# Smaller GpSimd pieces, half-tile turns of x and a fourth result buffer in a fused two-attention kernel

## The chip, the cores and the metric

The kernel runs on one core of one Trainium2 chip. A core has TensorE (PE in the profile), VectorE (DVE), ScalarE (ACT), GpSimd (POOL) and SyncE (SP), which here issues all DMAs. The metric is the device time of one execution in microseconds. The kernel before took 917.41 us, the median of three runs (917.04 to 918.87).

## The reference, cut to what matters

One input x (2048 rows of 512, bfloat16) goes through two attentions of 32 heads with 16 columns each, and a gate mixes them:

```
g = sigmoid((x * gate_w).sum(-1))
a = softmax(q k^T / 4) v @ wo            # full attention, weights A
b = softmax over 8 keys at distance 0, 2, .. 14, then @ wo    # local, weights B
out = g * a + (1 - g) * b
```

Both q, k and v come from x @ wqkv, with weights of their own. Part a needs 32 x 2048 x 2048 exponentials; part b only 32 x 2048 x 8.

## The kernel before, in words

**Loading and turning x.** x comes in four tiles of 512 rows (`load_x`), A's weights after the first tile. TensorE turns each x tile (`tr`, 16 transposes of 128 x 128, eight in each half of the columns) into PSUM, and two copies bring it to SBUF as `xTs[0]` and `xTs[1]` (`ev`: the first half on ScalarE, the second on VectorE). The PSUM tile `pxt` of an x tile takes 4 KB of a partition, in place `rA` for the even tiles and `rB` for the odd.

**PSUM.** Its eight banks are named: `rA` (three banks) and `rB` (two), the two score rings; `acc` (one), the running result of part a; and two `misc` banks, which every other product passes through.

**Part a.** The work is cut in 32 periods: a block of 512 queries (`c_`) and a group of four heads (`i`). A period has 64 units (16 key blocks of 128 times four heads), each a score tile of 128 keys x 512 queries. Three to five units of a period (`n_dve`) get their exponential on VectorE, the rest on ScalarE, in sets of three and two units by turns: `qk` writes the scores of a set into ring `rA` or `rB`, `ex` takes the exponential of the whole set into a `pT` buffer, and `pv` multiplies it with V and adds to `acc`, for two sets at a time (`pairs`). `pT` has three buffers a ring (`p_bufs`). K of a group is projected by `k_proj` and its row maxima taken (`km`) and joined (`selk`); q of a period by `q_proj`; V by `v_proj`. For group 0 ScalarE copies K (`kc`), otherwise VectorE. At a period's end VectorE transposes `acc` (`po1`), divides by the row sums and transposes back.

**VectorE's exponential.** `d_group` takes units one or two together. For each, `chain_of` has a score matmul into `misc` (`dq`) and four VectorE steps, `p1` to `p4`: `p1` writes `dt` (two buffers), `p2` reads `dt` twice (misc<-dt in the profile), `p3` and `p4` follow, and `p4` writes a `pd` tile of two units (four buffers), which is freed when its `pv` has read it.

**Part b.** For each of 16 blocks of 128 rows, `b_tile` projects q, k, v, writes k and v to DRAM and reads eight shifted copies of each back (`ksh`, `vsh`). GpSimd then multiplies and adds in a buffer `prod`: `logits_half` twice, then softmax on VectorE and ScalarE, then `av_half` twice. Its pieces are at most `HB` = 512 columns. The blocks are due 46.7 us apart (`b_space`), beginning at 32 us (`b_start`).

**The order.** Every step is an `op` with an engine, an estimated length, a due time, the steps that it depends on and the buffers that it takes and uses (`tok`). `list_schedule` plays these out once, when the program is built, and gives each engine a fixed order; PSUM banks and buffers go by that plan. An engine runs its order strictly in sequence, so a step that is held holds those behind it. The planner also puts filler matmuls of zeros (`zero`, the rows acc<-ones_t,z) where TensorE would be idle for long in its plan (`COVER`, `SPAN`). `rel` is a time in the plan before which a step does not start.

**The end.** The two results are projected with wo, mixed and written out in tiles of 128 rows; the last four wait for the last period.

All instructions but TensorE's carry one line, 280 (the helper that chains an engine's order); matmuls have 289, the turns of x 480. So the readings go by tile names.

Of the kernel before, what the change touches and what calls it, by code (L numbers as in the profile page):

```python
# [9 lines left out]
ALU = mybir.AluOpType  # L10
# [8 lines left out]
    set_sizes=(3, 2),  # L19
    n_dve=(3,) * 2 + (4,) * 14 + (5,) * 16,  # L20
    dve_tiles=2,
    p_bufs=3,
    pairs=True,
    cover=0.68,
    force=1.0,
    d_slack=2.0,
    d_lead=4.0,
    d_early=5.0,
    pd_bufs=4,
    q_bufs=3,  # L30
    shift=6.0,
    hold=0.3,
# [19 lines left out]
QW = 512  # L52
# [168 lines left out]
def kernel(  # L221
# [46 lines left out]
    def chain(bi):  # L268
        return chain_on("pe", bi)
# [199 lines left out]
    o_xt = []  # L469
    for sc in range(NC):  # L470
        st = {}
        tk = tok("rA" if sc % 2 == 0 else "rB", 1)

        def tr(half, sc=sc, st=st):
            def s():
                if half == 0:
                    st["p"] = ps.tile([128, DC, QW], BF16, tag=("rA" if sc % 2 == 0 else "rB"), bufs=1, name="pxt")
                for c in range(2 * half, 2 * half + 2):
                    for tt in range(TPC):
                        chain(nc.tensor.transpose(out=st["p"][:, c, tt * 128:(tt + 1) * 128],  # L480
                                                  in_=xld[sc][:, tt, c * 128:(c + 1) * 128], identity=ident[:]))
            return s

        def ev(half, sc=sc, st=st):
            def s():
                dst = xTs[half][:, :, sc * QW:(sc + 1) * QW]
                src = st["p"][:, 2 * half:2 * half + 2, :]
                if half == 0:
                    A.copy(out=dst, in_=src)
                else:  # L490
                    V.tensor_copy(out=dst, in_=src)
            return s
        t1 = op("pe", 0.6, tr(0), -5.0 + sc, deps=[o_x[sc], o_id], alloc=[tk], use=[xtok[sc]])
        t2 = op("pe", 0.6, tr(1), -4.9 + sc, deps=[t1], use=[tk, xtok[sc]])
        o_xt.append([op("act", 1.0, ev(0), -5.0 + sc, deps=[t1], use=[tk]),
                     op("dve", 0.68, ev(1), -4.9 + sc, deps=[t2], use=[tk])])
    all_xt = [o for os_ in o_xt for o in os_]


# [14 lines left out]
    def k_proj(i, sc, tag, dl, rel=0.0):  # L514
        st = {}
        tk = tok(tag, 2 if tag == "misc" else 1)

        def part(c0, c1):
            def s():
                if c0 == 0:  # L520
                    st["pk"] = misc_ps([128, QW], tag=tag)
                for c in range(c0, c1):
                    mm_heads(st["pk"], c, 1, i, xTs[c // 2][:, c % 2, sc * QW:(sc + 1) * QW], c == 0, c == DC - 1)
            return s

        def kc():
            if i == 0:
                A.activation(out=kt_all[:, i, sc * QW:(sc + 1) * QW], in_=st["pk"][:], func=ACT.Identity, scale=rowc[:, 0:1],
                             bias=rowc[:, 1:2])
                return  # L530
            V.tensor_scalar(out=kt_all[:, i, sc * QW:(sc + 1) * QW], in0=st["pk"][:], scalar1=rowc[:, 0:1],
                            scalar2=rowc[:, 1:2], op0=ALU.mult, op1=ALU.add)

        def km():
            V.tensor_reduce(out=kmax_all[:, i, sc:sc + 1], in_=st["pk"][:], axis=AX.X, op=ALU.max,
                            apply_absolute_value=True)
        b = steps(part, tk, dl - 2.6, [o_two[1, min(i, 1)], o_init_d] + o_xt[sc], rel=rel, name=f"kp{i}.{sc}")[-1]
        if i == 0:
            o_kc0.append(op("act", 0.65, kc, dl, deps=[b, o_init_d], use=[tk]))
            return op("dve", 0.70, km, dl, deps=[b], use=[tk])  # L540
        c = op("dve", 0.81, kc, dl - 0.8, deps=[b], use=[tk])
        return op("dve", 0.70, km, dl, deps=[b, c], use=[tk])

    def selk(i, dl):
        def s():
            V.tensor_reduce(out=kmax[:, i:i + 1], in_=kmax_all[:, i, :], axis=AX.X, op=ALU.max)
            V.scalar_tensor_tensor(out=rowq[:, i:i + 1], in0=kmax[:, i:i + 1], scalar=rowc[:, 2:3], in1=rowc[:, 0:1],
                                   op0=ALU.mult, op1=ALU.add)
        o_selk[i] = op("dve", 0.40, s, dl, deps=o_kc[i])

    for i in range(NG):
# [35 lines left out]
            for t in range(tb, tb + TB):  # L587
                o_v[(h, t)] = c

    v_proj(0, 4, 0, 8, "acc", T0 + 2.0, rel=T0 - 2.0)  # L590
    v_proj(0, 4, 8, 8, "misc", T0 + 3.0, rel=T0 - 2.0)
    for h0, h1, pn in ((4, 8, 2), (8, 16, 4), (16, 24, 8), (24, 32, 12)):
        TB = 512 // ((h1 - h0) * DH)
        for tb in range(0, NT, TB):
# [35 lines left out]
        c = op("dve", 0.70, mg, dl - 0.8, deps=[b], use=[tk])  # L630
        o_q[pi] = op("dve", 0.80, ev, dl, deps=[c, o_selk[i]], use=[tk, tq])

    q_proj(0, "misc", 2.9)
    for pi in range(1, NP):
        q_proj(pi, "misc", S0[pi] - 8.0 - shift(pi), rel=S0[pi - 1] - 1.0 - shift(pi))

# [46 lines left out]
    o_kvd, o_obt = [], []  # L683
    obt_tiles, obt_tok = {}, {}
    WH = W // 2
    HB = D

    def b_tile(t):
        st = {}
# [101 lines left out]
        def av_half(hf):  # L791
# [23 lines left out]
                    if hf:  # L815
                        G.tensor_tensor(out=st["obb"][:, cs], in0=ob[:, cs], in1=prod[:, 0, cs], op=ALU.add)
            return s
        l0 = op("pool", 11.9, logits_half(0), tb + 8, deps=[lk, qa], alloc=[tlg], use=[tks, tqb], name=f"lg{t}")
        l1 = op("pool", 11.9, logits_half(1), tb + 18, deps=[l0], use=[tks, tqb, tlg])
        a = op("dve", 1.3, sm_pre, tb + 19, deps=[l1], use=[tlg])  # L820
        a = op("act", 0.45, sm_exp, tb + 18, deps=[a], use=[tlg])
        a = op("dve", 2.28, sm_post, tb + 21, deps=[a, o_g], use=[tlg])
        a0 = op("pool", 10.2, av_half(0), tb + 40, deps=[a, lv], alloc=[tob], use=[tlg, tvs])
        a1 = op("pool", 11.8, av_half(1), tb + 48, deps=[a0], alloc=[tbb], use=[tlg, tvs, tob])
        tk = tok("misc", 2)
        if cb not in obt_tok:
            obt_tok[cb] = tok("obt", 2)
# [115 lines left out]
    def d_group(pi, gr, lo, hi):  # L943
        c_, i = periods[pi]
        n = len(gr)
        st = {}
        tp = tok("pd", cfg["pd_bufs"])

        def chain_of(q_, t, j, dl):
            tx, td = tok("misc", 2), tok("dt", 2)  # L950

            def dq():
                st["x"] = ps.tile([128, QW], FP32, tag=f"misc{bank[0]}", bufs=1, name="misc")
                mm(st["x"][:], kt_all[32 * j:32 * j + 32, i, t * 128:(t + 1) * 128], qt_tiles[pi][32 * j:32 * j + 32, :],
                   True, True, tile_position=(32 * j, 0))

            def p1():
                st["dt"] = work.tile([128, QW], FP32, name="dt", tag="dt", bufs=2)
                V.tensor_scalar(out=st["dt"][:], in0=st["x"][:], scalar1=float(DH) ** -0.5 * BITS / LN2,
                                scalar2=127.0 * BITS, op0=ALU.mult, op1=ALU.add)  # L960
                st["fr"] = st["dt"][:].bitcast(U16).rearrange("p (n two) -> p n two", two=2)[:, :, 0]

            def p2():
                V.scalar_tensor_tensor(out=st["x"][:], in0=st["fr"], scalar=EXP_A, in1=st["fr"],
                                       op0=ALU.subtract, op1=ALU.mult)

            def p3():
                V.scalar_tensor_tensor(out=st["x"][:], in0=st["fr"], scalar=EXP_R, in1=st["x"][:],
                                       op0=ALU.add, op1=ALU.mult)

            def p4():
                if q_ == 0:
                    st["pd"] = work.tile([128, 2, QW], BF16, name="pd", tag="pd", bufs=cfg["pd_bufs"])
                V.scalar_tensor_tensor(out=st["pd"][:, q_, :].bitcast(U16), in0=st["x"][:], scalar=EXP_C,
                                       in1=st["dt"][:], op0=ALU.mult, op1=ALU.add)
            a = op("pe", 0.20, dq, dl - 3.6, rows=True, deps=[o_q[pi], o_kc[i][t // TPC] if i else o_kc0[t // TPC]],
                   after=[d_last[0]], alloc=[tx], use=[q_tok[pi]], rel=lo, lat=0.47, name=f"dq{pi}")
            a = op("dve", 0.70, p1, dl - 2.3, deps=[a], alloc=[td], use=[tx])
            a = op("dve", lambda t_: 1.0 if in_b(t_) else 0.72, p2, dl - 1.4, deps=[a], use=[td, tx])
            a = op("dve", 0.70, p3, dl - 0.7, deps=[a], use=[td, tx])  # L980
            d_last[0] = op("dve", 0.70, p4, dl, deps=[a], alloc=[tp] if q_ == 0 else [],
                           use=[td, tx] + ([tp] if q_ else []), slack=cfg["d_slack"])

        def pv():
            for q_, (t, j) in enumerate(gr):
                pv_mm(pi, t, j, st["pd"][:, q_, :], vp_all[:, t])
        for q_, (t, j) in enumerate(gr):
            chain_of(q_, t, j, hi - 1.0 - 3.5 * (n - 1 - q_))
        a = d_last[0]
        o_pv[pi].append(op("pe", 0.23, pv, max(hi, S0[pi] + 5.0), deps=[a, o_t0[pi]] + [o_v[(4 * i + j, t)] for t, j in gr],  # L990
                           use=[tp, acc_tok[pi]], name=f"dpv{pi}",
                           sums=[((pi, j_), sum(1 for x in gr if x[1] == j_), NT) for j_ in sorted(set(x[1] for x in gr))]))
# [161 lines left out]
```

## Time and profile before

| what | value |
|---|---|
| median of three runs | 917.41 us |
| the profiled execution: its time, its span | 922.18 us, 920.4 us |
| mean granted clock of TensorE | 0.968 |
| ScalarE busy | 879.1 us, 96% |
| TensorE matmul busy | 787.0 us, 86% |
| VectorE busy | 717.5 us, 78% |
| GpSimd busy | 634.3 us, 69% |
| first exponential of part a starts | 21.19 us |
| last exponential ends | 911.76 us |
| last GpSimd instruction ends | 824.5 us |

The profile shows one execution. Its groups are told by output<-input tile, with the count, busy us, the mean length of one and the idle time of the engine just before them. The waits list who ended which engine's idle time. The slices cut the span in 40 parts of 23 us. The timeline gives each instruction's start and length in us from the span's start, and after it, in brackets, the idle time of its engine before it and the releaser.

### The profile page before, as it was taken

What the parts mean: (1) busy time and instruction counts of PE and PEld (TensorE: products, weight loads), DVE (VectorE), ACT (ScalarE), POOL (GpSimd) and SP (SyncE); (2) the same over time, 40 slices, a digit from 0 to 9 for tenths busy, and PEclk for the clock granted to TensorE, in tenths of its full rate; (3) what the DMA queues carried; (4) which work ended last, traced back from release to release, by engine and by line L of the source; (5) the groups of instructions that cost most, each with busy time, mean ns of one, the idle gap of its engine ahead of it and who ended that gap; (6) DMA issues with size and microseconds to landing.
All of it is one profiled execution on the core that took longest, in us unless ns stands there. A gap on an engine that the chain in (4) does not pass through costs nothing.

```text
span 920.4 us, 18227 instructions
## 1 busy us (share of the span) xinstructions
PE 787.0 (86%) x7383; PEld 255.3 (28%) x7383; DVE 717.5 (78%) x1073; ACT 879.1 (96%) x789; POOL 634.3 (69%) x545
## 2 busy tenths in 40 slices
PE   7988898888889888888888888898888888888785
PEld 4223232223322233222222222212222222322221
DVE  5678878888878786979687899978789868487852
ACT  4999999999999999999989999989899999998996
POOL 4357839797969686969697697969697979280000
PEclk9999999999998999999999999969799998999999
DMA  8303011103110302020302131201121101000000
GB/s 272 108 2 104 1 59 47 58 1 104 47 58 1 104 26 79 30 75 2 116 13 84 44 104 58 98 6 65 40 58 47 47 1 47 2 1 1 1 18 28
DMA packets 43996, 47.35 MB, mean 51 GB/s; under 512 B 1876, under 2 KB 41348, under 8 KB 43912
## 3 DMA queue, kind: packets, MB, share of 16 engines
q1 hardware_dynamic: 43912, 46.19, 15.8%
q8 instruction: 57, 0.93, 0.4%
q14 instruction: 27, 0.22, 0.1%
HBM read 39.86 MB, written 6.33 MB: 50 GB/s over the span
## 4 chain that ended last, share of the span: by engine, by line
ACT 57%; issue 21%; PE 15%; DVE 6%; DMA 1%; SPq 0%; ACTq 0%; DVEq 0%
ACT pT L280 56%; PE ring L289 5%; PE acc L289 5%; PE misc_ps L289 3%; DVE misc L280 2%; ACT lg L280 1%; DMA xld<-in_A_x_dram 1%; DVE dt L280 1%; PE misc L289 1%; DVE pd L280 1%; DVE ott L280 0%; DVE accT L280 0%; DVE kmax_all L280 0%; ACT xT L280 0%; PE pxt L480 0%
## 5 line engine op out<-in xcount | busy, mean ns | idle before, releaser
L280 ACT ACTIVATE pT<-ring 128x1536 bf16<-128x1536 f32 x763 | 869.5, 1397 | 21.5 <-PE ring L289 11.8
L289 PE MATMUL ring<-qt,kt_all 32*128 32x512 bf16 x1906 | 307.6, 389 | 113.9 <-ACT pT L280 108.5
L280 POOL TENSOR_TENSOR prod<-prod 128x512 f32<-128x512 f32 (+1 forms) x208 | 263.8, 1280 | 6.3
L289 PE MATMUL acc<-pT,vp_all 128*17 128x512 bf16 (+1 forms) x1906 | 257.7, 396 | 1.5 <-DVE vp_all L280 1.0
L289 PEld LDWEIGHTS <-kt_all 32*128 32x128 bf16 x2048 | 116.7, 91 | 417.6 <-issue 411.2
L280 POOL TENSOR_TENSOR prod<-vsh,lg 128x512 f32<-128x512 bf16 x128 | 148.2, 1188 | 93.3 <-issue 76.6
L280 POOL TENSOR_TENSOR prod<-ksh,qb 128x512 f32<-128x512 bf16 x128 | 155.1, 1242 | 76.4 <-DMA ksh<-kv_scr 41.4
L280 DVE SCALAR_TENSOR_TENSOR misc<-dt 128x512 f32<-128x512 uint16 x142 | 155.6, 1095 | 4.1
L280 DVE TENSOR_SCALAR dt<-misc 128x512 f32<-128x512 f32 x142 | 97.1, 684 | 45.4 <-PE misc L289 44.0
L289 PE MATMUL acc<-ones_t,z 128*32 128x512 bf16 x284 | 103.6, 401 | 0.0
L280 DVE SCALAR_TENSOR_TENSOR misc<-dt,misc 128x512 f32<-128x512 uint16 x142 | 98.4, 693 | 4.1
L280 DVE SCALAR_TENSOR_TENSOR pd<-misc,dt 128x512 uint16<-128x512 f32 x142 | 97.7, 688 | 4.2
L289 PE MATMUL misc_ps<-xT,wtw 128*32 128x512 bf16 x1024 | 87.5, 391 | 1.5 <-DVE pd L280 0.8
L289 PEld LDWEIGHTS <-vp_all 128*17 128x17 bf16 (+1 forms) x2048 | 54.5, 89 | 117.9 <-issue 107.3
L289 PE MATMUL misc_ps<-bw,xT 128*32 128x512 bf16 x768 | 66.1, 394 | 1.0 <-DVE pd L280 0.7
L289 PE MATMUL misc<-qt,kt_all 32*128 32x512 bf16 x142 | 54.9, 387 | 2.9 <-DVE pd L280 2.9
L280 DVE STREAM_TRANSPOSE accT<-acc 128x512 f32<-128x512 f32 x32 | 22.7, 710 | 23.3 <-PE acc L289 23.2
L289 PEld LDWEIGHTS <-xT 128*32 128x32 bf16 (+1 forms) x1088 | 32.0, 96 | 30.2 <-issue 23.5
L289 PEld LDWEIGHTS <-z 128*32 128x32 bf16 x294 | 26.3, 97 | 34.6 <-issue 25.9
L280 DVE CAST kvs<-misc_ps 128x512 bf16<-128x512 f32 x32 | 21.9, 685 | 15.9 <-PE misc_ps L289 15.9
L289 PEld LDWEIGHTS <-wtw 128*32 128x32 bf16 x1024 | 24.7, 95 | 28.8 <-issue 17.5
L289 PE MATMUL acc<-pd,vp_all 128*17 128x512 bf16 x142 | 32.2, 391 | 0.0
(70 smaller groups left out, 442.1 us busy)
## 6 DMA issues: line engine op xcount, KB each, us to landing
ksh<-kv_scr SPq DMA_DIRECT2D x16, 1024.0 KB, 5.8
vsh<-kv_scr SPq DMA_DIRECT2D x16, 1024.0 KB, 6.7
kv_scr<-kvs SPq DMA_DIRECT2D x16, 256.0 KB, 2.0
xld<-in_A_x_dram SPq DMA_DIRECT2D x4, 512.0 KB, 7.7
out_dram<-osb SPq DMA_DIRECT2D x16, 128.0 KB, 1.7
bw<-in_B_wqkv_dram SPq DMA_DIRECT2D x1, 1536.0 KB
wraw<-in_A_wqkv_dram SPq DMA_DIRECT2D x2, 512.0 KB, 8.7
wv<-in_A_wqkv_dram SPq DMA_DIRECT2D x1, 512.0 KB, 9.0
```

Source lines behind the costliest of these rows:

```text
L280: return chain_on(key, f(*a, **k))
L289: return chain(nc.tensor.matmul(out, lhsT=lhsT, rhs=rhs, start=start, stop=stop, **kw))
```

## The change

- `HB` becomes 256: each GpSimd product or sum over 512 columns is two instructions of 256. The planner's lengths of the four GpSimd steps of a block change from 11.9, 11.9, 10.2, 11.8 to 9.9, 9.9, 9.3, 10.6 us.
- Each half of an x tile gets a PSUM tile of its own (2 KB a partition), in `rA`, `rB` and `acc` by turns, with one copy on ScalarE (first half) or VectorE (second half). All eight halves are due before the other work of the head.
- `pT` has four buffers a ring, `pd` three, `dt` one.
- Group 0's K copy on ScalarE depends on the row maximum (`km`), and `selk`'s second step is a tensor_scalar.
- The first V projection takes a `misc` bank instead of `acc`, the first q projection `rA` instead of `misc`, and V's two start half a microsecond later in the plan at the earliest.
- The planner's length of `p2` beside part b becomes 0.95 instead of 1.0.

```diff
-    p_bufs=3,
+    p_bufs=4,
...
-    pd_bufs=4,
+    pd_bufs=3,
...
+        halves = []
+        for half in range(2):
+            tag = ("rA", "rB", "acc")[(2 * sc + half) % 3]
+            tk = tok(tag, 1)
+
+            def tr(half=half, sc=sc, st=st, tag=tag):
+                st[half] = ps.tile([128, 2, QW], BF16, tag=tag, bufs=1, name="pxt")
+                for c in range(2):
+                    for tt in range(TPC):
+                        chain(nc.tensor.transpose(out=st[half][:, c, tt * 128:(tt + 1) * 128],
+                                                  in_=xld[sc][:, tt, (2 * half + c) * 128:(2 * half + c + 1) * 128],
+                                                  identity=ident[:]))
+
+            def ev(half=half, sc=sc, st=st):
+                dst = xTs[half][:, :, sc * QW:(sc + 1) * QW]
                 if half == 0:
-                    A.copy(out=dst, in_=src)
+                    A.copy(out=dst, in_=st[half][:])
                 else:
-                    V.tensor_copy(out=dst, in_=src)
...
+            t1 = op("pe", 0.55, tr, -8.0 + 0.1 * (2 * sc + half), deps=[o_x[sc], o_id], alloc=[tk], use=[xtok[sc]])
+            halves.append(op("dve", 0.68, ev, -8.0 + 0.1 * sc, deps=[t1], use=[tk]) if half else
+                          op("act", 1.0, ev, -8.0 + 0.1 * sc, deps=[t1], use=[tk]))
...
-            o_kc0.append(op("act", 0.65, kc, dl, deps=[b, o_init_d], use=[tk]))
-            return op("dve", 0.70, km, dl, deps=[b], use=[tk])
+            o_km = op("dve", 0.70, km, dl, deps=[b], use=[tk])
+            o_kc0.append(op("act", 0.78, kc, dl, deps=[o_km, o_init_d], use=[tk]))
+            return o_km
...
-    v_proj(0, 4, 0, 8, "acc", T0 + 2.0, rel=T0 - 2.0)
-    v_proj(0, 4, 8, 8, "misc", T0 + 3.0, rel=T0 - 2.0)
+    v_proj(0, 4, 0, 8, "misc", T0 + 2.0, rel=T0 - 1.5)
+    v_proj(0, 4, 8, 8, "misc", T0 + 3.0, rel=T0 - 1.5)
...
-    q_proj(0, "misc", 2.9)
+    q_proj(0, "rA", 2.9)
...
-    HB = D
+    HB = D // 2
...
-            tx, td = tok("misc", 2), tok("dt", 2)
+            tx, td = tok("misc", 2), tok("dt", 1)
...
-                st["dt"] = work.tile([128, QW], FP32, name="dt", tag="dt", bufs=2)
+                st["dt"] = work.tile([128, QW], FP32, name="dt", tag="dt", bufs=1)
```

## The prediction, made before the result was known

> **What bounds the kernel now.** I read the page first (share of each engine, the slices, the chain), then the waits of ScalarE, then the stretches with their granted clock, then the groups by form, and last the timeline of the first 22 us. From the page:
>
> ```profile
> span 920.4 us, 18227 instructions
> PE   7988898888889888888888888898888888888785
> ACT  4999999999999999999989999989899999998996
> PEclk9999999999998999999999999969799998999999
> ACT 57%; issue 21%; PE 15%; DVE 6%; DMA 1%; SPq 0%; ACTq 0%; DVEq 0%
> L280 ACT ACTIVATE pT<-ring 128x1536 bf16<-128x1536 f32 x763 | 869.5, 1397 | 21.5 <-PE ring L289 11.8
> ```
>
> ScalarE is the bound: 763 exponentials keep it busy for 869.5 of 920.4 us, and the change alters neither their number nor their shape. So only three places can move: the head, up to the first exponential at 21.19 us; the idle time between exponentials, 21.5 us in this row, of which 1.75 stand before the first; and the tail after the last one (911.76 to 920.4 us), whose steps are untouched. Head, gaps and tail are at most some 50 us together. What ended ScalarE's gaps:
>
> ```profile
> ACT pT L280 <- PE ring L289: 11.8, 19, 1.7
> ACT pT L280 <- PE acc L289: 7.8, 6, 2.5
> ```
>
> The columns are us in total, times, longest. "ring" is a wait for scores. "acc" is a wait for an older result to be used up: the exponential has its scores but no free pT buffer. Counting units along the timeline confirms it: at 844.71 us, for instance, the matmuls on the result three steps back on the same ring ended 0.1 us before, those on the result four steps back 5.9 us before. The other five, at 83.94, 463.88, 473.54, 501.63 and 790.69 us, show the same picture. The stretches at half clock:
>
> ```profile
> 274.30:284.40 10.10, 9.54 (x57) 1.95 (x57) 8.41 (x15) 8.14 (x9) 9.79 (x10) 0.50 0.01 2
> ...
> 602.00:618.90 16.90, 16.82 (x94) 2.97 (x97) 13.79 (x22) 14.27 (x14) 8.44 (x9) 0.50 0.00 0
> ...
> sum 53.70, PE 52.76 PEld 10.05 DVE 40.38 ACT 42.91 POOL 40.33; mean PE 7.54 PEld 1.44 DVE 5.77 ACT 6.13 POOL 5.76
> ```
>
> After the length come busy us of PE, PEld, DVE, ACT, POOL, then the clock. Seven such stretches last 53.7 us in all and ScalarE is busy for 42.91 of them: 10.8 us lost, most of the ring waits. VectorE and GpSimd by form (count, busy, mean ns), the third line from the window after 825 us, where GpSimd has stopped:
>
> ```profile
> L280 POOL TENSOR_TENSOR prod<-prod 128x512 f32<-128x512 f32 x176 | 239.6, 1376 | 3.8
> L280 POOL TENSOR_TENSOR prod<-prod 128x256 f32<-128x256 f32 x32 | 24.2, 757 | 2.5
> L280 DVE SCALAR_TENSOR_TENSOR misc<-dt 128x512 f32<-128x512 uint16 x15 | 10.6, 704 | 0.4
> L280 DVE SCALAR_TENSOR_TENSOR misc<-dt 128x512 f32<-128x512 uint16 x142 | 155.6, 1095 | 4.1
> ```
>
> The head, from the timeline (start, length, idle before and its releaser):
>
> ```profile
> 6.64 1.01 ACT L280 COPY xT<-pxt 128x1024 bf16<-128x1024 bf16 x1 [4.63 <-PE pxt L480]
> 7.69 0.69 DVE L280 COPY xT<-pxt 128x1024 bf16<-128x1024 bf16 x1 [0.76 <-ACT xT L280]
> 15.44 0.61 PE L480 MATMUL pxt<-ident,xld 128*128 128x128 bf16 x8 [1.57 <-ACT xT L280]
> 15.98 1.91 PE L289 MATMUL misc_ps<-xT,wtw 128*32 128x512 bf16 x32
> 18.86 1.00 DVE L280 SCALAR_TENSOR_TENSOR rowq<-kmax,rowc 128x1 f32<-128x1 f32 x1
> 19.89 0.81 DVE L280 TENSOR_SCALAR qt<-misc_ps,rowq,rowl 128x512 bf16<-128x512 f32 x1
> ```
>
> A tile of x is one PSUM tile for both halves, so its first copy waits for both halves' transposes, the second copy waits for the first, and at 13.8 us the last transposes wait 1.57 us for a copy of the half before them. All of it is on the chain that sets the first exponential.
>
> **The change part by part.**
>
> *Fourth pT buffer a ring.* The acc waits go; what is late next is the score matmul behind the block of PV matmuls, in PE's queue. With PE's order as it is: at 83.94 us the scores were ready when ScalarE fell idle, and the next ones come in time: 0.86 saved. 463.88: 0.17. 473.54 (half clock): the next scores issue at 474.67, done near 475.1, and the exponential after them would have started at 475.9: 0.8 of 2.27. 501.63: 0.87. 790.69: next scores at 791.8, some 0.75 of 1.11. 844.71: next scores could issue near 845.6 and start their exponential at 846.0 where 847.0 stands: 1.0 of 2.49. Sum 4.5. The order is planned anew and can keep or lose some of it: I take 4, ends 0 and 7.8 (a further buffer takes no time of its own).
>
> *Head.* Each half has its own place, and its copy waits for its own eight transposes only. TensorE then has, after x's second tile lands at 8.05 us, 48 transposes (6 x 0.5), four K projections (4 x 1.0) and the first q projection (1.0), about 8 us back to back: it ends near 16.1 where 17.9 stands. I follow the copies: halves 0 and 1 end at 6.8 (ScalarE) and 7.65 (VectorE), 2 and 3 at 9.7 and 9.95, 4 and 5 at 11.3 and 11.45, 6 and 7 at 12.8 and 12.95. The third place is free for half 5 at 9.8, so no transpose waits over 0.3 us. On VectorE the last row maximum (0.69) now runs before the q projection ends; then come kmax 0.16, rowq 1.00 (kept at that although its form changes, since GpSimd's copies of wraw still run to 19.85), magn 0.76 and qt 0.81. So qt ends near 18.7 against 20.70, and with the 0.49 us between qt and the exponential the first one starts near 19.2: 2.0 us saved. If the copies of different halves still followed each other, as the 7.69 line shows them do within one tile, each second copy would come 0.7 to 1 us later and the saving be 1.0. I take the 2.0: the 6.64 line shows a copy waiting for transposes that it doesn't read, so the wait is for the tile, and now there are two. Ends 0 and 3. K of group 0 waiting for its maximum costs nothing: the trace has that order already, its ScalarE copies idle behind kmax_all for 4.7 us. The V projection loses its acc bank for a misc one and the q projection takes rA; each is free by then (kt copies done near 16.6), and V's 1.1 us twice end before the scores' turn; its cover gone, 1.1 us.
>
> By the Trainium skill, PSUM — Partial Sum Buffer, section PSUM bank collisions raise a hardware error, only the same bank in the same 32-partition quadrant must not be used by two engines at once. The two halves of before lay in different 2 KB banks and were still copied one after the other, so the rule alone would give the 2.0, the serial row the 1.0.
>
> *GpSimd in pieces of 256.* Per tile of b: logits 2 x 9 instructions become 2 x 16, values 7 + 8 become 14 + 16: 33 to 62, 464 more in all. Price of a split: by the shortest ones (611 ns for 256 columns, 1256 for 512) nothing, by the means 2 x 757 - 1376 = 138 ns, so 0 to 64 us of GpSimd, at most 4 us a tile on 39.6, inside a spacing of 46.7 us. Its last piece ends at 824.5, nearly 90 us ahead of the end, and ScalarE never waits for it: 0, and if that cover went, the 4 us. I take 0 (the shortest rows are those without VectorE in the way). On VectorE, misc<-dt takes 1095 ns on the mean, 704 without GpSimd and 1815 at most, that is 704 plus about one GpSimd instruction: it waits for the rest of one. 142 x 0.39 = 56 us, and ott<-accT,rden (777 against 424 ns) 11 more. Half the piece, half the wait: 33 us less VectorE work. VectorE is not the bound; between exponentials TensorE waits for it some 6 us (misc<-pd 2.9, misc_ps<-pd 1.4, others), of which few reach ScalarE: I take 0.5, ends -1 and 3.
>
> *Buffers given back.* One dt instead of two: no chain's first step starts ahead of the previous chain's last in any of the 142, so 0. Three pd pairs instead of four: along the timeline 78 of 80 pairs find at most two still in use; those at 748.96 and 774.38 us find three and would hold VectorE 2.4 and 4.8 us. I take 0, since the acc transposes behind them are covered by a period of 27 us; uncovered, 7 us. The new costs and due times in the planner change the order alone.
>
> *Sum.* The profiled execution took 922.18 (span 920.4 and 1.8 around it); 922.18 - 4 - 2 - 0.5 = 915.7. The median shown is 917.41, 4.8 lower, which I put on half-clock time that varies by execution; the saving is the same there: 917.4 - 6.5 = 910.9, so **911**.
>
> **The rivals.**
>
> *A: the half clock takes it, and more.* The order of the matmuls is new, and with it where TensorE runs thin. A stretch costs ScalarE 10.8/53.7 = 0.2 us per us. Twice the stretches cost 10.8 more: 922, slower. It decides from 8 us of loss, some 41 us more of half clock. For it: the stretches stand at seven points that the 27 us period of the order does not explain, so a new order deals them anew. Against: the rule that places filler matmuls is not touched, and fewer are as likely as more. Chance 0.14.
>
> The Trainium skill, TensorE: Matmul & The Clock Gate, section What's actually happening, says that the clock is halved by a free-running activity window of 3413 ns. The trace agrees: the stretches last 10.2, 3.4, 3.4, 17.1, 10.2, 3.4 and 6.8 us, multiples of it.
>
> *B: the pT waits turn into ring waits.* PE's queue is in order, and a late PV block holds the next scores just as long. Then the head alone is gained: 915.4 to 916.4, the border of a change that can be told. For it: 3.3 of the 7.8 us go that way in my count already. Chance 0.14.
>
> *C: VectorE is held by the third pd pair* in the crowded second half and the acc transposes come late; its 7 us and its repetition eat all: 918 to 921. Chance 0.05.
>
> *D: the relief of VectorE counts,* with most acc and ring gaps outside half clock (some 7 us) closed and the head at 3: 903. Chance 0.07.
>
> **How the numbers follow.** My forecast (904.5 to 915) has 0.60, the rivals 0.14, 0.14, 0.05 and 0.07. Range 903 to 920: it holds the forecast, B, D and half of C, reaches towards A, and leaves out A's worse part and the rest of C, some 0.15. Runs of this kernel differ by 0.2% (917.04 to 918.87), so faster means below 915.6: forecast 0.60, D 0.07 and 0.05 of B, 0.72. Same, to 919.2: 0.09 of B, 0.02 of C and 0.02 of A, 0.13. Slower: 0.12 of A and 0.03 of C, 0.15.
>
> **What would show it.** Right: first exponential near 19.2 us, no copy of x waiting for another engine's copy, acc gone from ScalarE's waits, misc<-dt near 900 ns, GpSimd's 256-column adds near 650 ns. Wrong: ring waits outside half clock above 5 us, half-clock stretches over 90 us, VectorE idle behind acc<-pd, or GpSimd above 45 us a tile so that obt comes late.

## The result and the profile after

The changed kernel is slower: 924.98 us, the median of 17 runs (920.59 to 929.03), against 917.40 us before in the same runs (911.25 to 920.46). The ratio is 1.0086, with a 95% interval of 1.0066 to 1.0105. The forecast was 911.

The profile shows an execution of 920.59 us (span 918.8), the fastest of the 17, so it shows the loss at its smallest; a second profile, of 928.54 us, follows below. The profile of before shows 922.18 us, longer than each of the 17 runs of before here. So the two profiles tell where time went, and not by how much the kernels differ. The page of the first:

```profile
span 918.8 us, 18621 instructions
ACT  5999999999999999999999999999999899999996
POOL 4269979698969998999999979999999998700000
PEclk9999999899999999999999999999798869999998
ACT 23%; POOL 22%; issue 9%; PE 5%; DVE 1%; ACTq 0%; DVEq 0%; POOLq 0%
L280 ACT ACTIVATE pT<-ring 128x1536 bf16<-128x1536 f32 x763 | 869.9, 1407 | 20.6 <-PE ring L289 17.8
```

The exponentials are the same 870 us. New in the chain that ended last is POOL with 22% of the span, where before it had no share, and most low digits of the clock now stand in the slices from 640 us on. ScalarE's waits and TensorE's:

```profile
ACT pT L280 <- PE ring L289: 17.8, 24, 3.4
ACT xT L280 <- PE pxt L481: 7.0, 4, 4.0
ACT lg L280 <- DVE lg L280: 1.4, 2, 0.8
ACT pT L280 <- PE acc L289: 0.9, 1, 0.9
```

```profile
PE misc_ps L834 <- POOL obb L280: 6.2, 5, 2.7
```

The waits for a free pT (acc) have gone from 7.8 to 0.9 us, as forecast. In their place stands something that the trace of before does not have: TensorE waits for GpSimd, 6.2 us in five places, at the transposes of obb (line 834), the last step of a block of part b. GpSimd by tile (min/median/max ns), first after, then before:

```profile
L280 POOL TENSOR_TENSOR prod<-ksh,qb x256: 658/669/1184, 39.1 to 767.6; 128x256 f32<-128x256 bf16 x128
L280 POOL TENSOR_TENSOR prod<-vsh,lg x256: 632/641/1158, 69.9 to 792.3; 128x256 f32<-128x256 bf16 x128
L280 POOL TENSOR_TENSOR ob<-prod x32: 723/728/1158, 77.0 to 787.3; 128x256 f32<-128x256 f32 x32
```

```profile
L280 POOL TENSOR_TENSOR prod<-ksh,qb x128: 1142/1154/1673, 38.1 to 782.6; 128x512 f32<-128x512 bf16 x128
L280 POOL TENSOR_TENSOR prod<-vsh,lg x128: 1088/1097/1617, 73.4 to 817.8; 128x512 f32<-128x512 bf16 x128
L280 POOL TENSOR_TENSOR ob<-prod x16: 1262/1268/1519, 80.7 to 812.9; 128x512 f32<-128x512 f32 x16
```

Two halves take 2 x 669 = 1338 ns where one piece took 1154, 2 x 641 = 1282 where 1097, 2 x 728 = 1456 where 1268. Each split costs 184 to 188 ns. GpSimd is busy for 707.2 us where it was 634.3: 44.2 us a block where it was 39.6.

What one wait does is seen at 725 us. Rows of TensorE and ScalarE from the timeline, and then the busy time of PE, PEld, DVE, ACT and POOL in three stretches, with the clock:

```profile
725.94 0.29 PE L834 MATMUL misc_ps<-ident,obb 128*32 128x128 bf16 x8 [0.83 <-POOL obb L280]
728.90 0.41 PE L834 MATMUL misc_ps<-ident,obb 128*32 128x128 bf16 x8 [2.67 <-POOL obb L280]
729.96 1.45 ACT L280 ACTIVATE pT<-ring 128x1536 bf16<-128x1536 f32 x1 [3.36 <-PE ring L289]
```

```profile
722.00:725.50 3.50, 2.69 (x30) 0.80 (x26) 3.36 (x6) 3.50 (x5) 3.34 (x5) 1.00 0.43 142
725.50:729.00 3.50, 0.39 (x16) 0.22 (x16) 0.57 (x1) 1.10 (x2) 3.26 (x6) 0.99 0.45 159
729.00:742.60 13.60, 13.60 (x75) 2.54 (x76) 7.92 (x11) 11.17 (x10) 13.37 (x20) 0.50 0.01 1
```

The transposes stand in TensorE's queue, and the scores behind them are held until the transposes have run. For 3.5 us TensorE works 0.39 us, ScalarE falls idle for 3.36 us, and the clock is halved for 13.7 us. The last row has ScalarE idle for 2.4 us, of which 1.0 us is the end of that wait, so the half clock adds some 1.5 us. The wait reported as 2.67 us thus costs about 5. In all, half-clock stretches before the last exponential last 71.7 us against 54.6.

The section that the prediction cited from the Trainium skill (TensorE: Matmul & The Clock Gate, section What's actually happening) has the clock fall to half after an idle window of about 3.4 us. This fall, at 728.92 us, agrees as nearly as the trace can show it: in the 3.41 us before it TensorE is busy for 0.31 us. The other nine falls of this profile do not: before them TensorE is busy for 1.5 to 2.5 of the 3.41 us, so the clock falls here without an idle window too. Which measure of activity decides, no run here shows.

The head reached what was forecast: the first exponential starts at 18.87 us where it was 21.19, and each half's copy but one starts within 0.05 us of the end of its own transposes (5.97 us where 6.64 stood). VectorE's misc<-dt takes 923 ns on the mean where it took 1095. From the head's timeline:

```profile
5.97 1.01 ACT L280 COPY xT<-pxt 128x1024 bf16<-128x1024 bf16 x1 [3.96 <-PE pxt L481]
9.43 0.69 DVE L280 COPY xT<-pxt 128x1024 bf16<-128x1024 bf16 x1 [1.67 <-PE pxt L481]
16.59 0.27 DVE L280 TENSOR_SCALAR rowq<-kmax,rowc 128x1 f32<-128x1 f32 x1
18.87 3.71 ACT L280 ACTIVATE pT<-ring 128x1536 bf16<-128x1536 f32 x3 [1.70 <-PE ring L289]
```

### The profile page after: what moved, and what is told of

Read it like the earlier page. It is cut to its first block, busy times and chain, and to the rows that moved or that the text cites. A ratio compares the mean times of both kernels' runs of the same rounds, so it can differ in the third digit from the quotient of the medians.

```text
span 918.8 us, 18621 instructions
## 1 busy us (share of the span) xinstructions
PE 786.0 (86%) x7338; PEld 250.4 (27%) x7338; DVE 688.0 (75%) x1073; ACT 879.2 (96%) x789; POOL 707.2 (77%) x1009
## 4 chain that ended last, share of the span: by engine, by line
ACT 23%; POOL 22%; issue 9%; PE 5%; DVE 1%; ACTq 0%; DVEq 0%; POOLq 0%
ACT pT L280 23%; POOL prod L280 20%; PE acc L289 2%; PE ring L289 2%; POOL obb L280 1%; PE misc_ps L289 1%; POOL ob L280 1%; POOL lg L280 0%; DVE misc L280 0%; PE misc L289 0%; ACT lg L280 0%; DVE dt L280 0%; DVE pd L280 0%; DVE accT L280 0%; DVE qt L280 0%
## 5 line engine op out<-in xcount | busy, mean ns | idle before, releaser
L280 POOL TENSOR_TENSOR prod<-prod 128x256 f32<-128x256 f32 x384 | 288.5, 774 | 5.0
L289 PE MATMUL acc<-pT,vp_all 128*17 128x512 bf16 (+1 forms) x1906 | 262.8, 398 | 0.5 <-ACT pT L280 0.2
L280 POOL TENSOR_TENSOR prod<-ksh,qb 128x256 f32<-128x256 bf16 x256 | 176.8, 726 | 30.9 <-DMA ksh<-kv_scr 19.0
L280 POOL TENSOR_TENSOR prod<-vsh,lg 128x256 f32<-128x256 bf16 x256 | 168.7, 694 | 38.9 <-issue 28.9
L280 DVE SCALAR_TENSOR_TENSOR misc<-dt 128x512 f32<-128x512 uint16 x142 | 131.1, 923 | 4.2
L289 PE MATMUL acc<-ones_t,z 128*32 128x512 bf16 x228 | 84.5, 409 | 0.0
L289 PE MATMUL misc_ps<-bw,xT 128*32 128x512 bf16 x768 | 62.9, 393 | 0.0
L289 PE MATMUL acc<-pd,vp_all 128*17 128x512 bf16 x142 | 35.8, 406 | 0.0
L280 DVE TENSOR_SCALAR misc_ps<-misc_ps,magn 128x512 uint32<-128x512 uint32 x32 | 24.2, 755 | 14.5 <-PE misc_ps L289 14.3
```

Source lines behind the costliest of these rows:

```text
L280: return chain_on(key, f(*a, **k))
L289: return chain(nc.tensor.matmul(out, lhsT=lhsT, rhs=rhs, start=start, stop=stop, **kw))
```

## The experiments

The lateness is told against the plan. The planner's own start and end times of each step were written out for every kernel; the trace's times minus these are the lag. They are the plan's times, not the chip's, and only serve as the line from which to measure. The plan of the changed kernel keeps 6.5 to 10 us between GpSimd's last step of a block and the transposes of obb (18 in the last block). A wait arises where GpSimd's lag exceeds that of ScalarE (which paces TensorE) by more than this.

The four planned lengths of GpSimd's steps add up to 45.8 us a block before and 39.7 after. Measured, a block takes 39.6 before and 44.2 after. So the plan of before was cautious by 6 us, and that of after is short by 4.5, each block.

Ratios are to the kernel before, run beside each (its medians: 917.40 beside the changed kernel, 918.05 beside e1 to e4, 917.69 beside e5 to e9, 918.70 beside e10 to e13). The clock is the mean granted clock over a kernel's runs.

| kernel | pieces | planned block | filler share | us | ratio (95%) | clock |
|---|---|---|---|---|---|---|
| before | 512 | 45.8 | 0.68 | 917.4 | 1 | 0.974 |
| after | 256 | 39.7 | 0.68 | 925.0 | 1.0086 (1.0066 to 1.0105) | 0.957 |
| e1 | 512 | 39.7 | 0.68 | 917.7 | 0.9999 (0.9971 to 1.0028) | 0.963 |
| e2 | 256 | 45.8 | 0.68 | 909.8 | 0.9903 (0.9868 to 0.9938) | 0.972 |
| e7 | 512 | 45.8 | 0.68 | 909.3 | 0.9905 (0.9867 to 0.9943) | 0.974 |
| e9, reserve 9 us | 256 | 39.7 | 0.68 | 912.1 | 0.9930 (0.9904 to 0.9957) | 0.971 |
| e10 | 256 | 39.7 | 0.72 | 921.0 | 1.0026 (1.0007 to 1.0046) | 0.965 |
| e11 | 512 | 39.7 | 0.72 | 910.7 | 0.9930 (0.9904 to 0.9957) | 0.978 |
| e12 | 512 | 45.8 | 0.72 | 911.7 | 0.9930 (0.9903 to 0.9957) | 0.975 |

All but the first row have the head and the buffers of the change. The next four are the kernel before with one part:

| kernel | us | ratio (95%) | clock |
|---|---|---|---|
| e3, pieces of 256 alone | 915.9 | 0.9968 (0.9944 to 0.9993) | 0.977 |
| e4, short planned lengths alone | 916.7 | 0.9979 (0.9952 to 1.0007) | 0.972 |
| e5, head alone | 915.9 | 0.9969 (0.9944 to 0.9995) | 0.971 |
| e6, buffers alone | 915.3 | 0.9968 (0.9939 to 0.9997) | 0.966 |

**Pieces and planned lengths, apart (e1 to e4).** The first theory was that the slow pieces become waits because the plan takes them for short. The rivals: the new order of matmuls deals more half clock, or the pieces cost by themselves.

e1, to the changed kernel:

```diff
-    HB = D // 2
+    HB = D
```

> The changed kernel with GpSimd's pieces back at 512 columns and everything else as changed; the planned lengths of GpSimd's steps are untouched, so the order of every engine by steps is that of the changed kernel. Theory (GpSimd at 44 us a block against 39.7 in the plan runs late, and the transposes of obb hold TensorE's queue): GpSimd back to 39 to 40 us a block, the waits for obb gone (0 against 6.2 us), half-clock time 30 to 55 us, time 908 to 913 us. Rival (the new order of the matmuls itself deals more half clock, GpSimd has no part): the order is the same, so half-clock time stays near 70 us and the time at 921 to 926 us.

Half right. With the very order of the changed kernel, pieces of 512 take back 7.3 us, and the waits for obb are gone from TensorE's list. But the time is 917.7, not 908 to 913. So lateness explains half of the way to 910, and something in the short plan the other half, with GpSimd on time (631.6 us busy, 39.5 a block). ScalarE's waits in its profile of 918.0 us:

```profile
ACT pT L280 <- PE ring L289: 18.4, 27, 2.3
ACT pT L280 <- PE acc L289: 0.9, 1, 0.9
```

e2, to the changed kernel, `9.9, 9.9, 9.3, 10.6` back to `11.9, 11.9, 10.2, 11.8`:

```diff
-        l0 = op("pool", 9.9, logits_half(0), tb + 8, deps=[lk, qa], alloc=[tlg], use=[tks, tqb], name=f"lg{t}")
+        l0 = op("pool", 11.9, logits_half(0), tb + 8, deps=[lk, qa], alloc=[tlg], use=[tks, tqb], name=f"lg{t}")
...
```

> The changed kernel with pieces of 256 columns kept and the planned lengths of GpSimd's four steps put back to 11.9, 11.9, 10.2 and 11.8 us. Theory (the plan's short lengths turn the slow pieces into waits): GpSimd still near 44 us a block, but no wait for obb in TensorE's queue, 909 to 915 us. Rival (the slow pieces cost the time by themselves, through VectorE and GpSimd on the shared port, whatever the plan says): 919 to 925 us.

The theory's range. Four numbers that run nowhere, only in the planner, are worth 15 us. GpSimd is just as slow here (by form, count, busy, mean; the profile shows the slowest of its 8 runs, 916.73 us):

```profile
L280 POOL TENSOR_TENSOR prod<-prod 128x256 f32<-128x256 f32 x384 | 292.3, 786 | 5.0
L280 POOL TENSOR_TENSOR prod<-ksh,qb 128x256 f32<-128x256 bf16 x256 | 173.1, 713 | 43.8 <-DMA ksh<-kv_scr 33.8 <-DVE qb L280 3.6 <-DVE dt L280 3.0
```

but TensorE waits nowhere for it. The rival that small pieces cost by themselves falls.

e3, to the kernel before:

```diff
-    HB = D
+    HB = D // 2
```

> The kernel before with pieces of 256 columns alone; its planned lengths (45.8 us a block) and so its order by steps stay. Theory (lateness against the plan): GpSimd 44 us a block is still inside its planned 45.8, so 915 to 919 us, no different from before. Rival (the slow pieces cost by themselves): 921 to 926 us.

Within the theory's range, at its fast end: 0.3% faster with GpSimd busy 76 us longer (710.0 against 634.3). The plan of before has room for a 44 us block, and TensorE waits nowhere for obb. That the gain comes from misc<-dt, 913 ns here, is likely but not shown.

e4, the kernel before with the planned lengths of the change:

```diff
-        l0 = op("pool", 11.9, logits_half(0), tb + 8, deps=[lk, qa], alloc=[tlg], use=[tks, tqb], name=f"lg{t}")
+        l0 = op("pool", 9.9, logits_half(0), tb + 8, deps=[lk, qa], alloc=[tlg], use=[tks, tqb], name=f"lg{t}")
...
```

> The kernel before, pieces of 512 kept, with the planned lengths of the change alone (39.7 us a block). Theory: GpSimd's 39.7 us a block, as measured, fit this plan, so few waits for obb and 914 to 920 us. Rival (short planned lengths are enough to lose the time, since the plan then has no reserve): 921 to 926 us with waits for obb.

No difference that can be told. Short lengths that are true (39.7 planned, 39.5 measured) do no harm without the head and buffers of the change.

The lag of GpSimd at the end of a block, and of ScalarE at that block's transposes, in us against each kernel's own plan (minus is ahead):

| block | after | after, second profile | e1 | e2 |
|---|---|---|---|---|
| 4 | -2.3 / -4.8 | 0.6 / -1.9 | -1.9 / -0.8 | -1.1 / 0.4 |
| 8 | 1.8 / -7.6 | 7.1 / -3.1 | -4.4 / -2.2 | -4.1 / -0.4 |
| 11 | 1.9 / -6.2 | 8.5 / 3.0 | -0.3 / 2.1 | 3.6 / 4.1 |
| 13 | 9.6 / -1.4 | 16.8 / 7.8 | 1.6 / 2.2 | 3.6 / 3.6 |
| 14 | 10.8 / 6.0 | 18.3 / 10.7 | -0.3 / 4.5 | 3.1 / 3.7 |

In the changed kernel GpSimd's lag rises and falls (it is 8.1 ahead at block 9) and is largest at blocks 13 and 14. At block 8 it is 1.8 late while ScalarE is 7.6 ahead, 9.4 apart where the plan keeps 7.7: TensorE waits 1.66 us at 498 us. At block 13 they are 11.0 apart where it keeps 7.1: the wait at 725.

**The other parts alone (e5, e6, e7).** e7 is e2 with pieces of 512:

```diff
-    HB = D // 2
+    HB = D
```

e5 is e7 with the buffers of before (and VectorE's step planned at 1.0 us again instead of 0.95), so only the head is left of the change:

```diff
-    p_bufs=4,
+    p_bufs=3,
-    pd_bufs=3,
+    pd_bufs=4,
...
-            tx, td = tok("misc", 2), tok("dt", 1)
+            tx, td = tok("misc", 2), tok("dt", 2)
...
```

e6 is the kernel before with

```diff
-    p_bufs=3,
+    p_bufs=4,
-    pd_bufs=4,
+    pd_bufs=3,
...
-            tx, td = tok("misc", 2), tok("dt", 2)
+            tx, td = tok("misc", 2), tok("dt", 1)
...
```

> The kernel before with the head of the change alone (half tiles of x in three places, the K copy behind its maximum, the first q projection in rA, V's first in misc); pieces of 512, buffers and planned lengths as before. Theory: the first exponential at 18.5 to 19 us instead of 21.0 to 21.2, and the 2.3 us reach the end: 914 to 917 us beside 918 of before. Rival (the new order deals the half-clock stretches anew and outweighs 2 us): anywhere from 911 to 922 us, in step with the granted clock.

> The kernel before with the buffers alone: four pT a ring, three pd, one dt. Theory (waits for a free pT cost ScalarE 7 to 8 us, some 4 of which are real): acc under 1.5 us in ScalarE's waits, 912 to 915.5 us beside 918. Rival (the scores stuck behind the PV block take the place of the missing buffer): acc gone too, ring waits outside half clock up by as much, 916.5 to 919 us.

> The changed kernel with pieces of 512 and the planned lengths of before (45.8 us a block), so head and buffers alone; every engine's order by steps is that of the run with cautious lengths and pieces of 256 (909.8 us). Theory (with a reserve in the plan the size of the pieces hardly matters): 908 to 913 us. Rival (the small pieces themselves give time, since VectorE's misc<-dt waits 0.1 us less each): 914 to 918 us.

All three fall in their theory's range, e6 by 0.2 us. The head alone brings the first exponential to 18.60 us and 0.31% of the time (0.05 to 0.56), the buffers alone 0.32% (0.03 to 0.61), both together 0.95%. The range of e5's rival holds its theory's, so the time of e5 does not decide between them. In the profile of e6 ScalarE's waits are

```profile
ACT pT L280 <- PE ring L289: 8.4, 11, 1.7
ACT pT L280 <- PE acc L289: 0.3, 1, 0.3
```

against 11.8 and 7.8 before. This execution, 909.37 us, is the fastest of e6's 12, and that of before a slow one, so the rows alone do not show that acc waits never turn into ring waits. The times speak against it: e7, which has the buffers on top of e5's head, takes 909.3 us where e5 takes 915.9. e7 and e2 have the same order and differ by 0.5 us, which can't be told apart: with a plan that has room, the size of the pieces does not matter. Both beat the kernel before and the changed one.

**Room by another way (e9).**

```diff
-    g_slack=4.0,
+    g_slack=9.0,
```

> The changed kernel, pieces of 256 and short planned lengths kept, with the distance that the plan leaves behind each GpSimd step raised from 4 to 9 us. Theory (it is the missing reserve between GpSimd and the transposes of obb in TensorE's queue that costs the time): waits for obb gone or under 1 us, half clock back under 60 us, 909 to 915 us. Rival (short planned lengths crowd the blocks of part b in the plan, and that crowding costs the time): waits for obb gone too, but 918 us or more.

The time is as expected, 912.1, 13 us better than the changed kernel, with its short lengths kept. The expected mechanism is only half there: the waits for obb are still 5.1 us in its profile.

```profile
PE misc_ps L834 <- POOL obb L280: 5.1, 3, 2.7
```

At block 13 GpSimd is 7.4 us late and ScalarE 8.6 ahead, 16 apart where this plan keeps 11.5. ScalarE then falls idle for 3.6 us, as long as in the changed kernel, so the reserve puts the first waits off to 727 us and does not end them. At the last exponential ScalarE is 4 us ahead of its plan, where the changed kernel is 4 behind, and half clock in its profile is 44.4 us in all. How much of the 13 us is the reserve and how much the new order is not shown. The rival of crowding alone (918 or more) falls.

**The clock (e10, e11, e12).** Between runs of the kernel before, 77 beside the experiments, the time grows by 0.40 to 0.46 us for each 0.001 of clock lost (a straight line through time against clock). The changed kernel's 0.957 against 0.974 is then worth 7 to 8 us; the line through its own 17 runs has 0.25, which gives 4. The two go together, and neither line shows which causes which. The question is whether that is a new deal of thin places in the plan, which more fillers would close, or idle time that the plan doesn't know of. The plan of before holds 294 fillers, that of the changed kernel and e1 only 249, and the traces count as many. With the edit below it is 307 in e10 and e11; e7 has 265 and e12 295. In each, to the changed kernel, e1 and e7:

```diff
-    cover=0.68,
+    cover=0.72,
```

> The changed kernel with the planner's filler share (cover) at 0.72 instead of 0.68: 307 filler matmuls in the plan instead of 249, nothing else. If half clock that the fillers can prevent is what the change loses (granted clock 0.957 on the mean against 0.974 before, some 8 us): clock 0.97 or more and 914 to 919 us. If late GpSimd and the waits behind it are the cause, fillers in the plan do not help, since the idle time of TensorE is not in the plan: clock under 0.965, 921 us or more.

> The changed kernel with pieces of 512 columns (917.7 us, GpSimd on time but the planned lengths short) and the filler share at 0.72. If what is left between it and the cautious plan (909.3 us) is half clock in planned idle time: clock 0.972 or more, 909 to 913 us. If it is the missing reserve of the plan: 915 us or more.

> Head and buffers of the change, pieces of 512, planned lengths of before (909.3 us), and the filler share at 0.72: 295 fillers in the plan instead of 265. If fillers buy clock here: 0.978 or more and 904 to 908 us, the fastest of all. If they only fill: 908 to 912 us.

e10 lies at the border of its second case: 4 us better than the changed kernel, still slower than before, GpSimd still up to 8 us late and TensorE waiting 3.4 us for obb. e11 falls in its first case: the clock rises from 0.963 to 0.978 and the time to 910.7, so what e1 loses beside e7 goes with half clock that more fillers, in an order dealt anew, take away. e12 gains nothing over e7: with cautious lengths, more fillers change nothing that can be told.

**A second profile (e13).** The changed kernel again, unaltered.

> The changed kernel once more, for a second profile, since the first shows the fastest of its executions. If late GpSimd is the cause: waits for obb of 5 us or more in TensorE's queue and half-clock stretches of 65 to 90 us again, at least one of them starting within 4 us behind such a wait. If the first picture was chance: waits for obb under 3 us.

Between the two numbers: 4.5 us for obb, in three waits, the longest 2.4, and 3.4 us in two waits of ScalarE that go another way, the longer 1.9. Half clock is 92.2 us, a little over the range. One fall of the clock (503.2 us) comes inside the 2.4 us wait that ends at 503.74. From the waits of ScalarE and the timeline at 690 us:

```profile
ACT pT L280 <- PE ring L289: 22.0, 32, 2.1
ACT lg L280 <- DVE lg L280: 3.4, 2, 1.9
```

```profile
690.91 0.42 DVE L280 TENSOR_REDUCE mx<-lg 128x32 f32<-128x256 f32 x1 [2.62 <-POOL lg L280]
692.00 0.42 ACT L280 ACTIVATE lg<-lg 128x256 f32<-128x256 f32 x1 [1.89 <-DVE lg L280]
693.80 0.39 PE L289 MATMUL ring<-qt,kt_all 32*128 32x512 bf16 x3 [2.51 <-ACT pT L280]
```

GpSimd's logits are late, VectorE's queue waits 2.62 us for them, ScalarE's queue 1.89 us for VectorE, and TensorE 2.51 us for ScalarE. At 694.4 us the clock falls to half for 17.1 us. The same chain stands in the first profile at 684 us, with a fall at 688. So lateness of GpSimd reaches the bound by two ways, through obb in TensorE's queue and through lg in VectorE's and ScalarE's.

A count along both profiles, of the half-clock stretches that begin inside such a wait of over 0.5 us or within 2 us behind it: 27.3 of 71.7 us in the first, 44.4 of 92.2 in the second. The rest, 44.4 and 47.8 us, is no more than the 54.6 of before. In these two executions the added half clock thus stands behind late GpSimd.

## Why the prediction was wrong, and where it was right

- *ScalarE is the bound, only head, gaps and tail can move:* right.
- *Fourth pT buffer, 4 us:* right in mechanism. acc went from 7.8 to 0.9 us, and alone the buffers give 0.32%, 2.9 us, with a wide interval.
- *Head, 2.0 us:* right in mechanism, with luck in the size. 21.19 to 18.87 us, 2.3, and 0.31% alone, 2.8 us. From the second tile on the two halves are copied side by side, so the larger of the two values held. But rowq, kept at 1.00 us because GpSimd's copies still run (to 20.08 us here), took 0.27 as a tensor_scalar. Those 0.7 us were put at nothing, and without them the saving is some 1.6.
- *Buffers given back, 0:* no cost seen. e6 has them, and gains; a small loss inside that gain can't be told.
- *misc<-dt near 900 ns:* right, 923, and VectorE is busy 29.5 us less (688.0 against 717.5) where 33 was forecast. Its worth of 0.5 us can't be told apart; e3 as a whole gains 0.3%.
- *Price of a split, 0, bounded by 138 ns:* wrong, 184 to 188. The row of 256 columns that I took (611 ns at the shortest) is the step that a split leaves whole, with another pattern; after the change it still takes 612, and the new pieces 708 at the shortest and 724 on the median. (The shortest of 512 is 1248 ns in the trace, not 1256; that changes nothing.) The upper bound from the means mixed two shapes and two shares of waiting. A block grew by 4.6 us, over the 4 given as the most.
- *"0, and if that cover went, the 4 us":* the step that failed. The cover that I named was the spacing of 46.7 us and the 90 us behind GpSimd's last instruction. Neither is what TensorE's queue goes by. That is the planned end of each block, and I passed over it in the half sentence that new costs "change the order alone". The planned lengths went down by 6.1 us a block while the work went up by 4.6, and TensorE waited 6.2 us for obb where it had not waited at all. Nothing in the prediction set the measured 39.6 beside the planned 45.8 and 39.7, though both stood in front of me. With planned lengths put back, head and buffers give 909.3 and 909.8, against 911 forecast.
- *Rivals:* none was this one. A named the half clock, and much of the loss does show there (4 to 8 us, by the lines through time and clock). Against A stood that the filler rule is untouched; the number of fillers is not, it fell from 294 to 249. But the cause given, a new deal of the order, accounts for a part only: e1 and e11 show some 7 us of it, while e1 against after and e11 against e10 show 7 to 10 us for late GpSimd in unaltered orders. B is against the times of e7 and e5. Of C, none of VectorE's waits in the profile is for a pd buffer. D's 903 was reached by no kernel. "GpSimd above 45 us a tile so that obt comes late" stood among the signs of a wrong forecast; 44.2 was enough.

What stays open: how the loss divides between the waits and the half clock that follows them, since the one brings the other, and why true short lengths lose clock with the head and buffers of the change (e1) and not without them (e4). Each experiment that alters the plan also deals the order anew, so only after against e1, e10 against e11, e2 against e7 and before against e3 compare one order with itself.

## What to carry to other kernels

Where an order is planned from estimated lengths, a change of an estimate is a change of the kernel: set each estimate beside the measured length, before and after, and ask which in-order queue goes by it. An engine that is idle a quarter of the time can still hold the bound, if its result stands in the bound's queue with less room in front of it than it is late. And a row's shape must be that of the new instruction before its duration is used.

## What the runs showed of the hardware

- A GpSimd tensor_tensor of 256 columns takes 641 to 728 ns on the median where one of 512 takes 1097 to 1268, so half the columns are far from half the time. If the time grows in a straight line with the columns, 184 to 188 ns of it are fixed, an estimate from these rows. The Trainium skill, GPSIMD Engine Reference, section 2.1 Instruction dispatch, names one indirect call, tens of cycles, for the software dispatch of each instruction. How much of the fixed part that call is, no run here shows.
- A step of 256 elements whose inner run is two elements takes 612 ns at the shortest and 614 on the median; the same count in long runs takes 708 and 724.
- One stretch of 3.5 us in which TensorE works 0.39 us is followed by 13.7 us at half clock, in which ScalarE, fed by TensorE, is busy for 11.2 of 13.6 us. The other nine falls of the clock in that profile come behind 3.41 us with TensorE busy for 1.5 to 2.5.
- Runs of one kernel differ by 10 us (913.8 to 924.2 in the 31 runs of before beside e1 to e4), and the mean granted clock goes with it, from 0.983 to 0.960.
